# Regrouping the score tiles of a fused attention and mixer kernel from three tiled bursts a step into two

## Chip, cores, metric

One core of one Trainium2 chip. The metric is the device time of the program in microseconds (us), the median of several runs.

## The reference

Attention with squared ReLU in place of softmax, on 8 x 12 heads of 448 positions and 64 channels; its output, with heads side by side, is the input of a mixer block: two matmuls over the positions with a residual, then two over the channels with a residual.

```python
scores = scale * np.matmul(q, k.transpose(0, 1, 3, 2))
attn = np.maximum(scores, 0.0) ** 2 / S
x = (attn @ v) with heads side by side              # 8 x 448 x 768
xt = x.transpose(0, 2, 1)
h = np.maximum(xt @ w_tok1, 0.0) @ w_tok2           # token mixing, 448 -> 256 -> 448
u = x + h.transpose(0, 2, 1)
h2 = np.maximum(u @ w_ch1, 0.0) @ w_ch2             # channel mixing, 768 -> 1536 -> 768
return u + h2
```

## The kernel before

The work is cut into 24 steps of four heads. In a steady step PE computes the scores of step i, the values, token1 and token2 of step i-1, and fills in with channel-mixing units of finished batches. Scores, values and the q/k transposes use the array as four tiles of 64 x 64; everything else uses the whole array. A run of tiled work between full-array work is called a burst below. PE is TensorE, which multiplies matrices into PSUM; ACT (ScalarE) and DVE (VectorE) evict the results, that is, copy them out so that the PSUM buffer is free again; SP issues DMA transfers. x_sb is the transposed x that token1 reads. The parts that matter (cuts marked with `...`):

```python
ps_att = ... tile_pool(name="ps_att", bufs=2, space=PSUM)      # two score buffers of two banks each
ps_acc = ... tile_pool(name="ps_acc", bufs=1, space=PSUM)      # values, q/k transposes, token2
ps_mm  = ... tile_pool(name="ps_mm",  bufs=2, space=PSUM)      # token1, channel units

def scores(i, c):                       # one score tile: four 64x64 matmuls of 448 columns
    ps = ps_att.tile([128, 2, 512], FP32, tag="att", name="sc_ps")
    ...
    nc.scalar.activation(at, ps[:, :, :S], AF.Relu)            # ACT evicts it
    squares.append(at)                                         # DVE squares it later

def fill(share, least=0):               # channel units, paid from a credit
    if not queue:
        return
    credit[0] += share * rate[0]
    done = 0
    while queue and (credit[0] > 0 or done < least):
        cost, unit = queue.pop(0)
        credit[0] -= cost
        unit()
        done += 1
...
for i in range(DB + 1, ND + 2):         # DB = 3, ND = 24; steady from i = 7 on (slow is false)
    slow = i <= 2 * DB
    ...
    scores(i, 0); scores(i, 1)                                 # burst 1
    values(i - 1, range(QC)); values_out(i - 1)
    scores(i, 2)
    ...
    x_back(i - 1)                       # from step 9 on: a DMA transpose of x, needed by token1
    ... u_back(...)                     # DMA transposes of the residual, same SP queue
    square()
    fill(1 / 3)
    scores(i, 3); scores(i, 4)                                 # burst 2
    transposes(i + 1)
    square()
    fill(2 / 9)
    token1(i - 1)
    fill(1 / 9, least=1)
    scores(i, 5); scores(i, 6)                                 # burst 3
    token2(i - 1)
    ...
    square()
    fill(1 / 3)
```

A channel-1 unit is six matmuls evicted by ACT; a channel-2 unit is twelve matmuls evicted by DVE.

Of the kernel before, what the change touches and what calls it, by code (L numbers as in the profile page):

```python
# [16 lines left out]
def kernel(  # L17
# [19 lines left out]
    ND = B * H // 4  # L37
    DB = H // 4
# [88 lines left out]
    def transposes(i, place="acc", split=False):  # L127
        sb = attn.tile([128, 2, 2, S], BF16, name="qkT")
        if place == "att":
            both = ps_att.tile([128, 2, 1024], BF16, tag="att", name="qkT_ps")  # L130
            parts = [both[:, r] for r in range(2)]
        else:
            parts = [ps_acc.tile([128, 1024], BF16, tag=f"acc{r}", name="qkT_ps1") for r in range(2)]
        for w in (1, 0) if i == 0 else (0, 1):
            src = raws.pop((i, "qk"[w]))
            for c in range(QC):
                at = w * S + c * 64
                for r in range(2):
                    h = slice(64 * r, 64 * (r + 1))
                    for g in range(2):  # L140
                        nc.tensor.matmul(  # L141
                            parts[r][64 * g : 64 * (g + 1), at : at + 64],
                            lhsT=src[h, g, c, :],
                            rhs=ident[h, h],
                            is_transpose=True,
                            start=True,
                            stop=True,
                            skip_group_check=True,
                        )
        qkT[i] = sb  # L150
        if place == "att":
            nc.vector.tensor_copy(sb.rearrange("n r w t -> n r (w t)"), both[:, :, : 2 * S])
            return
        for r in range(2):
            (nc.scalar.copy if split and r == 0 else nc.vector.tensor_copy)(  # L155
                sb[:, r].rearrange("n w t -> n (w t)"), parts[r][:, : 2 * S]
            )

    def scores(i, c):
        sb = qkT[i]  # L160
        ps = ps_att.tile([128, 2, 512], FP32, tag="att", name="sc_ps")
        for r in range(2):
            for g in range(2):
                h = slice(64 * g, 64 * (g + 1))
                nc.tensor.matmul(  # L165
                    ps[64 * r : 64 * (r + 1), g, :S],
                    lhsT=sb[h, r, 1, c * 64 : (c + 1) * 64],
                    rhs=sb[h, r, 0, :],
                    start=True,
                    stop=True,  # L170
                    skip_group_check=True,
                )
        at = attn.tile([128, 2, S], BF16, name="at", bufs=12)
        nc.scalar.activation(at, ps[:, :, :S], AF.Relu)  # L174
        squares.append(at)
        at2[i, c] = at

    def square(keep=0):
        while len(squares) > keep:
            at = squares.pop(0)  # L180
            nc.vector.tensor_tensor(out=at, in0=at, in1=at, op=ALU.mult)  # L181
# [38 lines left out]
    x_tiles, r1_tiles, uT_tiles = {}, {}, {}  # L220
    XDMA = 8
# [28 lines left out]
    def token1(i):  # L250
        x_sb = x_tiles.pop(i)
        ps = ps_mm.tile([128, JC, 256], FP32, tag="bank", name="t1_ps")
        for j in range(JC):
            for c in range(4):
                nc.tensor.matmul(  # L255
                    ps[:, j, :],
                    lhsT=wt1[:, c, j * 128 : (j + 1) * 128],
                    rhs=x_sb[:, :, c, :],
                    start=(c == 0),
                    stop=(c == 3),  # L260
                )
        r1 = mix.tile([128, JC, 256], BF16, name="r1_sb")
        nc.scalar.activation(r1, ps, AF.Relu)  # L263
        r1_tiles[i] = r1

    def token2(i, early=False, rs=(0, 1)):
        b, d = divmod(i, DB)
        if d == 0 and b % 2 == 0 and 0 in rs:
            uT_tiles[b // 2] = mix.tile([128, NP, 2 * S], BF16, name="uT_sb")
        r1 = r1_tiles[i]  # L270
        off = (b % 2) * S
        if early:
            parts = {r: ps_mm.tile([128, 512], FP32, tag="bank", name="h_ps1") for r in rs}
        else:
            parts = {r: ps_acc.tile([128, 512], FP32, tag=f"acc{r}", name="h_ps") for r in rs}
        for r in rs:
            for j in range(JC):
                nc.tensor.matmul(  # L278
                    parts[r][:, :S],
                    lhsT=r1[:, j, r * 128 : (r + 1) * 128],  # L280
                    rhs=wt2[:, j, :],
                    start=(j == 0),
                    stop=(j == JC - 1),
                )
        for r in rs:
            nc.vector.tensor_tensor(  # L286
                out=uT_tiles[b // 2][:, 2 * d + r, off : off + S],
                in0=parts[r][:, :S],
                in1=xT[b % 2][:, 2 * d + r, :S],
                op=ALU.add,  # L290
            )
        if 1 in rs:
            u_later.append(i)
# [3 lines left out]
    u_later = []  # L297
# [5 lines left out]
    def u_back(i):  # L303
        b, d = divmod(i, DB)
        t = chunks(b)
        if b not in u_tiles:
            u_tiles[b] = mix.tile([128, NP, NT - NT // 2, 128], BF16, name="u_sb", bufs=3)
        for p in (2 * d, 2 * d + 1):
            nc.sync.dma_start_transpose(
                out=u_tiles[b][:, p, : len(t), :],  # L310
                in_=uT_tiles[b // 2][:, p, t.start * 128 : t.stop * 128],
            )

    def hold_back(b, src):

        u_tiles[b] = mix.tile([128, NP, NT - NT // 2, 128], BF16, name="u_sb", bufs=3)
        for p in range(NP):
            nc.gpsimd.tensor_copy(u_tiles[b][:1, p, 0, :1], src)
# [76 lines left out]
    def channel_work(b):  # L395
        for e in range(2 if b == 0 else 0, EC):
            queue.append((C1, lambda e=e: channel1(b, e)))
        for t in chunks(b):
            for j in range(2):
                later.append((C2, lambda t=t, j=j: channel2(b, t, j)))  # L400
        if b > 0:
            queue.extend(later)
            later.clear()
# [6 lines left out]
    def fill(share, least=0):  # L410
# [9 lines that stand above are left out]
# [74 lines left out]
    i = DB  # L494
# [31 lines left out]
    for i in range(DB + 1, ND + 2):  # L526
        slow = i <= 2 * DB
        if i == 2 * DB + 1:
            rate[0] = (EC * C1 + NT * C2) / DB
        if i < ND:  # L530
            scores(i, 0)
            scores(i, 1)
        if 0 <= i - 1 < ND:
            values(i - 1, range(QC))
            values_out(i - 1)
        if i < ND:
            scores(i, 2)
        if i - 1 < XDMA:
            fill(1 / 3, least=1)
        if 0 <= i - 1 < ND:  # L540
            x_back(i - 1)
        if i > 2 * DB + 1:
            if i == 2 * DB + 2:
                hold_back(1, x_tiles[i - 1][:1, 0, 0, :1])
            while u_later and u_later[0] < i - 1:
                u_back(u_later.pop(0))
        if i + PRE < ND:
            if i - 1 >= XDMA:
                nc.gpsimd.tensor_copy(gate, x_tiles[i - 1][:1, 1, 3, 127:])  # L549
            load_four(i + PRE)  # L550
        if i == 5:
            load_wc2(1, 2)
        square()
        if i - 1 >= XDMA:
            fill(1 / 3)
        if i < ND:
            scores(i, 3)
            scores(i, 4)
        if i + 1 < ND:
            transposes(i + 1)  # L560
        square()
        if not slow:
            fill(2 / 9)
        if 0 <= i - 1 < ND:
            token1(i - 1)
        fill(1 / 3 if slow else 1 / 9, least=1)
        if i < ND:
            scores(i, 5)
            scores(i, 6)
        if 0 <= i - 1 < ND:  # L570
            token2(i - 1)
            if (i - 1) % DB == DB - 1:
                channel_work((i - 1) // DB)
            if i == 2 * DB + 1:
                hold_back(0, uT_tiles[1][:1, 0, :1])
                for _ in range(DB):
                    u_back(u_later.pop(0))
        square()
        fill(1 / 3, least=1 if slow else 0)
    while queue:  # L580
        queue.pop(0)[1]()

# [29 lines left out]
```

## Time and profile before

| | before |
|---|---|
| median time | 380.68 us (380.0 to 380.86) |
| span of the profiled run | 377.8 us |
| PE busy | 365.5 us, 97% |
| DVE, ACT busy | 205.9 us, 213.4 us |
| PE waiting for a score buffer from 76 to 332 us | never |
| PE waiting for x_sb there | 1.4 us in two waits |

PE is the bound and hardly waits in the steady steps. In a timeline row the columns are the start in us, the length in us, engine, line, operation, out<-in, shapes and the count of merged instructions, then in brackets the idle time before it and what ended that.

### The profile page before, as it was taken

The page shows a single profiled execution, that of the slowest core. Times are in us where ns is not written, and L with a number is a line of the kernel's source. Part 1 is how long each engine was busy: PE and PEld are TensorE (multiplying, and loading weights), DVE is VectorE, ACT ScalarE, POOL GpSimd, SP SyncE. Part 2 cuts the span into 40 slices and gives each one's busy share as a digit, 9 for nine tenths or more (in the row PEclk, how much of TensorE's full clock was granted, in tenths as well). Part 3 has the DMA queues.
Part 4 walks back from the last instruction along what each step waited for, and adds up shares of the span by engine and source line. Part 5 has one row for each costly group of instructions (what it writes and reads, how often), then busy time and mean ns, then how long its engine had stood idle before and what let it go on. Part 6 is the DMA issues. An engine that isn't in the chain of part 4 may idle for free.

```text
span 377.8 us, 10082 instructions
## 1 busy us (share of the span) xinstructions
PE 365.5 (97%) x4335; PEld 200.7 (53%) x4335; DVE 205.9 (54%) x371; ACT 213.4 (56%) x297; POOL 100.9 (27%) x186
## 2 busy tenths in 40 slices
PE   8888999999989999999999999999999999999995
PEld 3444455555555564565555554555545654555563
DVE  2876688764567665465555575466555664121021
ACT  4996888877434457745676347654676446412400
POOL 8974548212330321430321304303300000000000
PEclk9999999999999999999999999999999999999999
DMA  8989999933988866846835898738550344333024
GB/s 153 121 118 203 193 206 170 183 45 71 150 146 163 160 137 111 108 79 136 154 65 72 146 139 139 112 61 171 97 103 17 74 115 87 57 69 85 0 61 107
DMA packets 69325, 43.30 MB, mean 115 GB/s; under 512 B 43360, under 2 KB 65824, under 8 KB 69280
## 3 DMA queue, kind: packets, MB, share of 16 engines
q0 software_dynamic: 24416, 21.47, 39.8%
q1 hardware_dynamic: 44560, 20.75, 26.0%
q8 instruction: 34, 0.56, 0.6%
q10 hardware_dynamic: 304, 0.43, 0.4%
q14 instruction: 11, 0.09, 0.1%
HBM read 43.38 MB, written 11.01 MB: 144 GB/s over the span
## 4 chain that ended last, share of the span: by engine, by line
PE 88%; DVE 4%; ACT 4%; DMA 3%; issue 1%; SPq 0%; ACTq 0%
PE m_ps L327 28%; PE m_ps L366 27%; PE sc_ps L165 9%; PE acc_ps L193 8%; PE t_ps L255 6%; PE h_ps L278 5%; DMA x_sb<-xT 3%; ACT at L174 3%; PE qkT_ps L141 3%; DVE uT_sb L286 1%; PE warm_ps L429 1%; DVE at L181 1%; PE m_ps L345 1%; DVE xT L211 1%; PE x_ps L237 1%
## 5 line engine op out<-in xcount | busy, mean ns | idle before, releaser
L174 ACT ACTIVATE at<-sc_ps 128x896 bf16<-128x896 f32 x168 | 145.1, 920 | 59.3 <-PE sc_ps L165 59.0
L327 PE MATMUL m_ps<-uT_sb,wc 128*128 128x448 bf16 x564 | 115.6, 353 | 0.2 <-DVE uT_sb L286 0.2
L366 PE MATMUL m_ps<-wc,r_sb 128*128 128x384 bf16 x672 | 115.2, 326 | 0.0
L181 DVE TENSOR_TENSOR at<-at 128x896 bf16<-128x896 bf16 x168 | 96.8, 619 | 7.6 <-ACT at L174 7.6
L366 PEld LDWEIGHTS <-r_sb 128*128 128x128 bf16 x672 | 64.3, 98 | 45.6 <-issue 3.9
L334 ACT ACTIVATE r_sb<-m_ps 128x448 bf16<-128x448 f32 x94 | 51.2, 544 | 60.1 <-PE m_ps L327 59.8
L327 PEld LDWEIGHTS <-wc 128*128 128x128 bf16 x564 | 53.3, 98 | 49.8 <-issue 4.3
L373 DVE TENSOR_TENSOR out_sb<-m_ps,u_sb 128x384 f32<-128x384 f32 x56 | 31.1, 556 | 60.6 <-PE m_ps L366 59.6
L165 PE MATMUL sc_ps<-qkT 64*64 64x448 bf16 x672 | 52.7, 360 | 2.9 <-ACT at L174 2.2
L286 DVE TENSOR_TENSOR uT_sb<-h_ps,xT 128x448 bf16<-128x448 f32 x48 | 27.8, 620 | 39.5 <-PE h_ps L278 39.5
L211 DVE TENSOR_SCALAR xT<-acc_ps 128x448 bf16<-128x448 f32 x45 | 26.1, 620 | 34.8 <-PE acc_ps L193 34.8
L193 PE MATMUL acc_ps<-at,v_raw 64*64 64x448 bf16 x672 | 38.6, 350 | 0.0
L549 POOL COPY gate<-x_sb 1x1 bf16<-1x1 bf16 x12 | 2.3, 193 | 126.2 <-DMA x_sb<-xT 126.2
L83 POOL DMA_DIRECT2D q_raw<-in_q_dram x48 | 29.0, 615 | 20.0 <-DMA wc<-in_moe_w_ch_dram 16.9
L165 PEld LDWEIGHTS <-qkT 64*64 64x64 bf16 x672 | 15.6, 105 | 30.8 <-issue 26.6
L83 POOL DMA_DIRECT2D v_raw<-in_v_dram x48 | 29.5, 636 | 7.2 <-DMA wc<-in_moe_w_ch_dram 4.6
L155 DVE COPY qkT<-qkT_ps 128x896 bf16<-128x896 bf16 x39 | 22.6, 619 | 14.9 <-PE qkT_ps L141 14.9
L83 POOL DMA_DIRECT2D k_raw<-in_k_dram x46 | 28.1, 630 | 0.1
L255 PE MATMUL t_ps<-x_sb,wt 128*128 128x256 bf16 x192 | 25.0, 273 | 2.1 <-DMA x_sb<-xT 1.4
L193 PEld LDWEIGHTS <-v_raw 64*64 64x64 bf16 x672 | 20.2, 107 | 12.1 <-issue 0.8
L263 ACT ACTIVATE r_sb<-t_ps 128x512 bf16<-128x512 f32 x24 | 14.3, 597 | 20.7 <-PE t_ps L255 20.6
L278 PE MATMUL h_ps<-wt,r_sb 128*128 128x448 bf16 x96 | 22.6, 355 | 0.0
(40 smaller groups left out, 122.0 us busy)
## 6 DMA issues: line engine op xcount, KB each, us to landing
out_dram<-out_sb SPq DMA_DIRECT2D x54, 192.0 KB, 3.3
q_raw<-in_q_dram POOLq DMA_DIRECT2D x48, 112.0 KB, 4.3
v_raw<-in_v_dram POOLq DMA_DIRECT2D x48, 112.0 KB, 5.4
k_raw<-in_k_dram POOLq DMA_DIRECT2D x46, 112.0 KB, 5.5
wc<-in_moe_w_ch_dram POOLq DMA_DIRECT2D x4, 1152.0 KB, 11.0
u_sb<-uT_sb SPq DMA_TRANSPOSE x48, 2.6
x_sb<-xT SPq DMA_TRANSPOSE x16, 3.3
k_first<-in_k_dram SPq DMA_DIRECT2D x1, 224.0 KB, 3.5
```

What stands on the lines that cost most here:

```text
L83: eng.dma_start(out=dst[64 * r : 64 * (r + 1)].rearrange("p g c d -> p g (c d)"), in_=src[b, h0 : h0 + 2].rearrange("g (p c) d -> p g (c d ...
L165: nc.tensor.matmul(ps[64 * r : 64 * (r + 1), g, :S], lhsT=sb[h, r, 1, c * 64 : (c + 1) * 64], rhs=sb[h, r, 0, :], start=True, stop=True, s ...
L174: nc.scalar.activation(at, ps[:, :, :S], AF.Relu)
L181: nc.vector.tensor_tensor(out=at, in0=at, in1=at, op=ALU.mult)
L193: nc.tensor.matmul(ps[r][64 * g : 64 * (g + 1), :S], lhsT=v_raw[h, g, c, :], rhs=at[h, g, :], start=(c == 0), stop=(c == QC - 1), skip_gro ...
L255: nc.tensor.matmul(ps[:, j, :], lhsT=wt1[:, c, j * 128 : (j + 1) * 128], rhs=x_sb[:, :, c, :], start=(c == 0), stop=(c == 3),)
L278: nc.tensor.matmul(parts[r][:, :S], lhsT=r1[:, j, r * 128 : (r + 1) * 128], rhs=wt2[:, j, :], start=(j == 0), stop=(j == JC - 1),)
L286: nc.vector.tensor_tensor(out=uT_tiles[b // 2][:, 2 * d + r, off : off + S], in0=parts[r][:, :S], in1=xT[b % 2][:, 2 * d + r, :S], op=ALU.add,
L327: nc.tensor.matmul(ps[:, :S], lhsT=wc1[:, g, e * 128 : (e + 1) * 128], rhs=uT[:, g, off : off + S], start=(g == 0), stop=(g == CC - 1),)
L334: nc.scalar.activation(r2[:, e, off : off + S], ps[:, :S], AF.Relu)
L366: nc.tensor.matmul(ps[:, :HN], lhsT=r2[:, e, t * 128 : (t + 1) * 128], rhs=wc2[:, e, cols], start=(e == 0), stop=(e == EC - 1),)
L373: nc.vector.tensor_tensor(out=o[:, cols].rearrange("n (g d) -> n g d", d=128), in0=ps[:, :HN].rearrange("n (g d) -> n g d", d=128), in1=u_ ...
```

## The change

The intent is to leave and enter tiled mode twice a step instead of three times: score 3 joins the first burst, score 6 goes behind the transposes, scores 4 and 5 stand ahead of them. Fill shares are redistributed (they still sum to 1 a step, but to 4/3 in steps 7 and 8). A second part issues one pair of residual transposes a step later, so that fewer of them stand in the SP queue ahead of the first x transpose.

```diff
--- before.py
+++ after.py
@@ -535,6 +535,8 @@
             values_out(i - 1)
         if i < ND:
             scores(i, 2)
+            if not slow:
+                scores(i, 3)
         if i - 1 < XDMA:
             fill(1 / 3, least=1)
         if 0 <= i - 1 < ND:
@@ -542,7 +544,7 @@
         if i > 2 * DB + 1:
             if i == 2 * DB + 2:
                 hold_back(1, x_tiles[i - 1][:1, 0, 0, :1])
-            while u_later and u_later[0] < i - 1:
+            while u_later and u_later[0] < max(i - 1 - (i == 2 * DB + 2), 0):
                 u_back(u_later.pop(0))
         if i + PRE < ND:
             if i - 1 >= XDMA:
@@ -551,19 +553,39 @@
         if i == 5:
             load_wc2(1, 2)
         square()
-        if i - 1 >= XDMA:
-            fill(1 / 3)
+        if not slow:
+            fill(0.45, least=2)
+            if i < ND:
+                scores(i, 4)
+                scores(i, 5)
+            if i + 1 < ND:
+                transposes(i + 1)
+            if i < ND:
+                scores(i, 6)
+            square()
+            fill(0.1)
+            if 0 <= i - 1 < ND:
+                token1(i - 1)
+            fill(0.1, least=1)
+            if 0 <= i - 1 < ND:
+                token2(i - 1)
+                if (i - 1) % DB == DB - 1:
+                    channel_work((i - 1) // DB)
+            if i == 2 * DB + 1:
+                hold_back(0, uT_tiles[1][:1, 0, :1])
+                for _ in range(DB):
+                    u_back(u_later.pop(0))
+            fill(0.35)
+            continue
         if i < ND:
             scores(i, 3)
             scores(i, 4)
         if i + 1 < ND:
             transposes(i + 1)
         square()
-        if not slow:
-            fill(2 / 9)
         if 0 <= i - 1 < ND:
             token1(i - 1)
-        fill(1 / 3 if slow else 1 / 9, least=1)
+        fill(1 / 3, least=1)
         if i < ND:
             scores(i, 5)
             scores(i, 6)
@@ -571,12 +593,8 @@
             token2(i - 1)
             if (i - 1) % DB == DB - 1:
                 channel_work((i - 1) // DB)
-            if i == 2 * DB + 1:
-                hold_back(0, uT_tiles[1][:1, 0, :1])
-                for _ in range(DB):
-                    u_back(u_later.pop(0))
         square()
-        fill(1 / 3, least=1 if slow else 0)
+        fill(1 / 3, least=1)
     while queue:
         queue.pop(0)[1]()
 
```

## The prediction

> **What bounds the kernel now.** I read the page first, then PE's waits in the steady stretch, then the timelines of PE and ACT over one steady step. The page:
>
> ```profile
> PE 365.5 (97%) x4335; PEld 200.7 (53%) x4335; DVE 205.9 (54%) x371; ACT 213.4 (56%) x297; POOL 100.9 (27%) x186
> PEclk9999999999999999999999999999999999999999
> ...
> L174 ACT ACTIVATE at<-sc_ps 128x896 bf16<-128x896 f32 x168 | 145.1, 920 | 59.3 <-PE sc_ps L165 59.0
> L334 ACT ACTIVATE r_sb<-m_ps 128x448 bf16<-128x448 f32 x94 | 51.2, 544 | 60.1 <-PE m_ps L327 59.8
> ```
>
> PE is busy for 97% of the span at full clock. No other engine passes 56%, so PE's instruction stream sets the time: a microsecond that PE idles or loses is a microsecond of the kernel. ACT needs 920 ns per score tile (168 of them, seven per step) and 544 ns per channel-1 unit. PE's waits between 76 and 332 us, which hold the steady steps but for the first few microseconds of the first, are a single row:
>
> ```profile
> PE t_ps L255 <- DMA x_sb<-xT: 1.4, 2, 1.2
> ```
>
> So now PE never waits for a score buffer there. It waits twice for a residual transpose (1.19 us at 109 us, 0.24 us at 227 us). That no score wait exists is the fact that the change puts at risk. The PE timeline of one steady step:
>
> ```profile
> 166.26 0.57 PE L165 MATMUL sc_ps<-qkT 64*64 64x448 bf16 x8
> 166.66 0.39 PE L141 MATMUL qkT_ps<-ident,q_raw 64*64 64x64 bf16 x28
> 166.88 0.43 PE L141 MATMUL qkT_ps<-ident,k_raw 64*64 64x64 bf16 x28
> 167.25 2.12 PE L366 MATMUL m_ps<-wc,r_sb 128*128 128x384 bf16 x12
> 169.21 1.04 PE L255 MATMUL t_ps<-x_sb,wt 128*128 128x256 bf16 x8
> 170.11 2.11 PE L366 MATMUL m_ps<-wc,r_sb 128*128 128x384 bf16 x12
> 172.15 0.57 PE L165 MATMUL sc_ps<-qkT 64*64 64x448 bf16 x8
> 172.65 0.93 PE L278 MATMUL h_ps<-wt,r_sb 128*128 128x448 bf16 x4
> 173.42 2.11 PE L366 MATMUL m_ps<-wc,r_sb 128*128 128x384 bf16 x12
> 175.46 0.57 PE L165 MATMUL sc_ps<-qkT 64*64 64x448 bf16 x8
> 175.87 1.49 PE L193 MATMUL acc_ps<-at,v_raw 64*64 64x448 bf16 x28
> 177.19 0.36 PE L165 MATMUL sc_ps<-qkT 64*64 64x448 bf16 x4
> ```
>
> Three tiled (64*64) bursts a step stand between full-array work. The reader should look at starts, because the ends are modelled. Twelve m_ps matmuls followed by more full-array work take 1.96 us (167.25 to 169.21); followed by a burst they take 2.04 us (170.11 to 172.15). Individual starts in the trace give 256 against 163 ns for the last one: 0.09 us to enter a burst. Two score tiles followed by tiled work take 0.40 us (166.26 to 166.66); followed by full-array work 0.50 us (172.15 to 172.65): 0.10 us to leave. A burst costs about 0.195 us besides its work. The ACT timeline gives when score buffers come free:
>
> ```profile
> 160.79 2.53 ACT L174 ACTIVATE at<-sc_ps 128x896 bf16<-128x896 f32 x3
> 166.70 1.73 ACT L174 ACTIVATE at<-sc_ps 128x896 bf16<-128x896 f32 x2 [3.38 <-PE sc_ps L165]
> ```
>
> With ACT idle the first eviction starts 0.44 us after the score tile does (166.26 to 166.70) and takes 0.92, so its buffer is free at +1.35; the second follows 0.81 later, free at +2.17 (0.44 + 1.73). If the work before the burst was a channel-1 unit, ACT evicts that first: the burst of 160.24 had its first eviction start at 160.79, 0.55 after, and everything is 0.11 later (+1.46 and +2.27). There are only two score buffers, and the startup shows what happens when they run out:
>
> ```profile
> 14.65 0.38 PE L165 MATMUL sc_ps<-qkT 64*64 64x448 bf16 x4
> 15.46 0.38 PE L165 MATMUL sc_ps<-qkT 64*64 64x448 bf16 x4
> 16.27 0.38 PE L165 MATMUL sc_ps<-qkT 64*64 64x448 bf16 x4
> ```
>
> Score tiles then start every 0.81 us, ACT's pace, each 0.05 us after the end of the eviction of two tiles earlier.
>
> **What the Trainium skill says.** "TensorEngine Tiling (Array Packing)", section Key Properties: a change of tiling mode drains the array. The trace agrees: 0.09 us in, 0.10 us out. "TensorE: Matmul & The Clock Gate", section Step-by-step: only weight loads are pulled ahead, the matmuls stay in program order. So a score tile that waits holds back all full-array work behind it; the startup rows fit that. "ScalarE: Activation LUTs", section What ACT_TABLE_LOAD costs: an activation with immediates takes 186 ns plus 0.833 ns per element, and neighbours overlap by about 93 ns. For 896 elements that is 932 and 839 ns; the trace has 920 and 0.81 us. "Perfetto Trace Analysis", section Optimization Strategy: the same gap repeating on the engine that should be saturated can mean too few buffers. The trace before has no such gap; I expect the one after to have it.
>
> **The change part by part.** Steps i = 7 to 23 (17 of them) go from bursts of three score tiles around the values, two ahead of the transposes, and two alone, to: scores 0 and 1, values, scores 2 and 3; and scores 4 and 5, transposes, score 6. PE's matmuls are the same in number and shape, only reordered; the order listing of the changed program confirms that, and that scores 2 and 3 each carry a wait on ACT.
>
> Removed: one burst a step. 17 x 0.195 = 3.3 us saved.
>
> Added, first burst, counted from its start: scores 0 and 1 take 0.40, values 1.32, score 2 starts at 1.73 (buffer 0 free at 1.35 or 1.46: no wait, as today). Score 3 would start at 1.94, but its buffer is free at 2.17 + 0.05 = 2.22, or 2.32 after a channel-1 unit. PE waits 0.28 or 0.38 us. Working the fill credit through the program gives a channel-1 unit just before this burst in 11 of the 17 steps, a channel-2 unit (evicted by DVE) in 6: 11 x 0.38 + 6 x 0.28 = 5.9 us.
>
> Added, second burst: scores 4 and 5 take 0.40, transposes 0.48, so score 6 could start at 0.88. Buffer 4 is free at 1.35 + 0.05 = 1.40, or 1.51 after channel 1. PE waits 0.52 or 0.63. The credit gives 11 steps after channel 2 and 5 after channel 1; in step 23 there are no transposes, so score 6, ready at 0.43, waits until 1.51, that is 1.08. 11 x 0.52 + 5 x 0.63 + 1.08 = 9.9 us.
>
> Moved: the fill shares still sum to 1.0 a step (four thirds in steps 7 and 8, so a few channel units run earlier and the tail holds fewer; the same PE work). The queue never empties in the steady part in either version. In five steps the 0.1 fill ahead of token1 is empty, so token1 follows score 6 directly. Its x_sb must have landed by then: two channel-2 units (3.9 us) and the second burst still stand between, token1 starts about 6.3 us after the end of the values, and the transposes land 4.4 to 4.7 us after it in most steps (6.0 and 6.6 in two with heavy loading). So little is lost there.
>
> Residual transposes: at step 8 one pair fewer is queued on SP ahead of step 9's x_sb transpose, whose issue today falls 1.64 us after the values instead of 1.25, landing late. With that, and with more PE work between, the two waits for x_sb go: 1.4 us saved.
>
> Sum: -3.3 - 1.4 + 5.9 + 9.9 = +11.1 us, all on PE and so on the path. 380.68 + 11.1 gives 391.8 us, 2.9% slower.
>
> **The rivals.** (a) The author's hope: values and transposes give ACT time to free the buffers, so waits vanish and only the burst saving counts: 380.7 - 3.3 - 1.4 = 376.0 us. Against it: the buffer of score 1 comes free at +2.17 after the burst's start, in today's trace, while score 3 would be due at +1.94; and 0.48 us of transposes do not cover the 0.92 us of an eviction. For it: only that the pauses in the design were put where ACT needs them. (b) Burst waits half as long as I count, because something that I take as lost (the drain into full-array work, the wait for x_sb) hides inside them: +15.8 x 0.5 - 4.7 = +3.2, 384 us. Against it: starts alone were used, and the drain comes after score 6, not in its wait. (c) More waits than I count: token2's weights wait for r1, which ACT now evicts behind scores 5 and 6. I get r1 ready at about 3.55 us after the second burst's start and token2 due at 3.7 where only one channel-1 unit stands between: 0.15 us of room. If it misses by 0.5 us in the five steps with the empty fill, or x_sb lands late there, +2 to 3 us: 394 us.
>
> **Range and chances.** The waits come from start times and durations that repeat from step to step within 0.02 us, so the sum is good to some 2 us either way if the mechanism holds: 388.5 to 394.5 us. A slowdown of over 2% needs more than 388.3 us, that is 70% of my net sum; I give it 0.86. Within 2%: 0.12, mostly (b). Faster by 2% is beyond even (a): 0.02.
>
> **What would show it.** PE's waits should have a new row, score tiles waiting for ACT's evictions, about 34 times and near 16 us in total, none of them over 1.1 us; PE's busy share falls to some 93%, with PE's busy time down by about 2 to 4 us. Score 3 should start 2.2 to 2.3 us and score 6 1.4 to 1.5 us after their burst's first tile. x_sb's row should be gone from the waits of PE. I am wrong if that score row is under 8 us, if the saving per burst is not near 0.2 us, or if a row of token2 waiting for r1, or of token1 for x_sb, exceeds 2 us.

## The result

The changed kernel takes 391.37 us (391.17 to 391.69, four runs) against 380.56 us before (380.0 to 380.86) in the same rounds: a ratio of 1.0286, 95% interval 1.0269 to 1.0304. Ratios here are the mean time of one kernel's fast runs over that of the other's fast runs of the same rounds, so not quite the ratio of the medians that are quoted. The profiled spans are 389.8 and 377.8 us; they differ by more than the medians because the profiled run of the kernel before took 379.59 us, less than any of the four runs of its median.

The page after, with PE's busy share and the two groups concerned (the number after the second bar is the idle time of the engine just before these instructions):

```profile
PE 367.8 (94%) x4335; PEld 205.4 (53%) x4335; DVE 206.7 (53%) x371; ACT 211.6 (54%) x297; POOL 99.8 (26%) x186
...
L174 ACT ACTIVATE at<-sc_ps 128x896 bf16<-128x896 f32 x168 | 143.1, 924 | 65.5 <-PE sc_ps L165 65.2
...
L165 PE MATMUL sc_ps<-qkT 64*64 64x448 bf16 x672 | 56.0, 361 | 13.3 <-ACT at L174 12.0
```

PE runs the same 4335 matmuls in a longer span. The idle time ahead of the score matmuls was 2.9 us before, all in the startup; now it is 13.3 us, 12.0 of it ended by ACT's evictions in waits of over 0.15 us. ACT itself is idle for longer than before (65.5 against 59.3 us ahead of its evictions): it is late in each burst without being busy overall.

PE's waits after, from 76 to 345 us (total us, times, longest):

```profile
PE sc_ps L165 <- ACT at L174: 9.4, 27, 0.9
PE m_ps L366 <- DVE out_sb L373: 0.3, 1, 0.3
PE m_ps L327 <- ACT r_sb L334: 0.2, 1, 0.2
```

The row for x_sb has gone and a row for score buffers has come. One steady step after, PE:

```profile
171.97 0.57 PE L165 MATMUL sc_ps<-qkT 64*64 64x448 bf16 x8
172.38 1.49 PE L193 MATMUL acc_ps<-at,v_raw 64*64 64x448 bf16 x28
173.70 0.87 PE L165 MATMUL sc_ps<-qkT 64*64 64x448 bf16 x8
174.50 4.07 PE L366 MATMUL m_ps<-wc,r_sb 128*128 128x384 bf16 x24
178.51 0.57 PE L165 MATMUL sc_ps<-qkT 64*64 64x448 bf16 x8
178.91 0.39 PE L141 MATMUL qkT_ps<-ident,q_raw 64*64 64x64 bf16 x28
179.13 0.43 PE L141 MATMUL qkT_ps<-ident,k_raw 64*64 64x64 bf16 x28
179.91 0.38 PE L165 MATMUL sc_ps<-qkT 64*64 64x448 bf16 x4 [0.35 <-ACT at L174]
```

and ACT in the same stretch:

```profile
172.41 3.43 ACT L174 ACTIVATE at<-sc_ps 128x896 bf16<-128x896 f32 x4 [4.33 <-PE sc_ps L165]
178.94 1.73 ACT L174 ACTIVATE at<-sc_ps 128x896 bf16<-128x896 f32 x2 [3.10 <-PE sc_ps L165]
```

Scores 2 and 3 (the row at 173.70) need 0.80 us from start to the next full-array matmul at 174.50, where two score tiles used to take 0.50 (172.15 to 172.65 in the prediction's timeline). Score 6 starts at 179.91, 1.40 us after its burst's first tile, though the transposes begin at 178.91 and take 0.48 us. The chain of work that ended last (start, length, what) passes through ACT at this place, where before it stayed on PE:

```profile
178.58 0.34 PE sc_ps L165 x4
178.92 0.02 issue
178.94 0.93 ACT at L174
179.87 0.04 issue
179.91 0.38 PE sc_ps L165 x4
```

One reading trap: the idle time in the wait row is smaller than what PE lost. Score 3 has an idle time of 0.13 or 0.23 us, but from score 2's start to score 3's start there are 0.49 or 0.59 us where 0.21 would do (the time between the first two tiles of a burst). The modelled end of the tile before counts the first 0.16 us or so of each wait as busy: for 34 waits 5.4 us, which less the 3.3 us of the saved bursts is near the 2.3 us by which PE's busy time rose with the same work. The six waits of 0.13 us are missing from the row altogether.

### The profile page after: what moved, and what is told of

Same layout as the page of the kernel before. It is cut to its first block, busy times and chain, and to the rows that moved or that the text cites.

```text
span 389.8 us, 10078 instructions
## 1 busy us (share of the span) xinstructions
PE 367.8 (94%) x4335; PEld 205.4 (53%) x4335; DVE 206.7 (53%) x371; ACT 211.6 (54%) x297; POOL 99.8 (26%) x186
## 4 chain that ended last, share of the span: by engine, by line
PE 76%; ACT 11%; issue 6%; DVE 3%; POOL 2%; DMA 1%; ACTq 0%; POOLq 0%; DVEq 0%
PE m_ps L366 28%; PE m_ps L327 28%; ACT at L174 10%; PE sc_ps L165 7%; PE t_ps L255 5%; PE h_ps L278 4%; PE acc_ps L193 2%; DVE uT_sb L286 1%; DVE at L181 1%; POOL q_raw L83 1%; DMA wt<-in_moe_w_tok_dram 1%; PE m_ps L345 1%; PE qkT_ps L141 1%; ACT x_sb L246 1%; POOL wt L96 1%
## 5 line engine op out<-in xcount | busy, mean ns | idle before, releaser
L174 ACT ACTIVATE at<-sc_ps 128x896 bf16<-128x896 f32 x168 | 143.1, 924 | 65.5 <-PE sc_ps L165 65.2
L165 PE MATMUL sc_ps<-qkT 64*64 64x448 bf16 x672 | 56.0, 361 | 13.3 <-ACT at L174 12.0
L165 PEld LDWEIGHTS <-qkT 64*64 64x64 bf16 x672 | 20.5, 104 | 43.4 <-issue 38.1
```

The source lines that it names most:

```text
L165: nc.tensor.matmul(ps[64 * r : 64 * (r + 1), g, :S], lhsT=sb[h, r, 1, c * 64 : (c + 1) * 64], rhs=sb[h, r, 0, :], start=True, stop=True, s ...
```

## The experiments

My theory was that of the prediction: PE waits for score buffers behind ACT, against a small saving per burst. The rivals were that the transposes' new place on the SP queue, the redistributed fill, or something in longer bursts made the difference.

### One part of the change alone: the residual transposes

```diff
 (kernel before)
-            while u_later and u_later[0] < i - 1:
+            while u_later and u_later[0] < max(i - 1 - (i == 2 * DB + 2), 0):
```

> The kernel before with only the residual transposes spread by a step (three bursts kept). My theory: only the 1.19 us wait of token1 for x_sb in step 9 goes, so about 379.4 us, 0.3% faster than before; the 0.24 us wait of step 17 stays. Rival (the spread of transposes is what made the changed kernel slow, by pushing DMA work into step 9): slower than before by several us.

Measured: 379.25 us against 379.74 before, ratio 0.9982 (0.9966 to 0.9998). The direction fits. The gain is smaller than the 1.2 us that I expected: 0.5 us by the medians and by the spans (377.3 against 377.8); the interval, 0.02 to 0.34%, just holds the expected 0.3%. The mechanism fits only in part. PE's waits from 76 to 345 us:

```profile
PE t_ps L255 <- DMA x_sb<-xT: 1.0, 1, 1.0
```

The transpose of step 9 was issued 1.25 us after the values instead of 1.64, as expected, yet it took 4.93 us to land, where most x transposes take 3.2 to 3.3. So the wait shrank from 1.19 to 0.95 us and did not go. In this run step 17's wait of 0.24 us was gone instead.

### The other part alone: the bursts

```diff
 (kernel after)
-            while u_later and u_later[0] < max(i - 1 - (i == 2 * DB + 2), 0):
+            while u_later and u_later[0] < i - 1:
```

> The changed kernel with the residual transposes issued as before, so only the two bursts and the fill shares differ from before. My theory: 391.4 us, the same as the changed kernel within 0.3 us, because token1 of step 9 now starts 8.3 us after the values and x_sb lands 6.4 us after them. Rival: at least 1 us away from the changed kernel, in either direction.

Measured: 391.60 us, ratio to before 1.0306; span 389.7 against 389.8 us for the whole change, with the same row of score waits (9.4 us, 27 times). Bursts and fill make the whole difference; the spread of the transposes is worth nothing in the changed kernel, because token1 there comes late enough anyway: in step 9 of this run x_sb landed 2.8 us ahead of it.

### Score 3 alone, and the last-but-one tile behind the transposes alone

```diff
 (kernel before; first run)                     (kernel before; second run)
             scores(i, 2)                                    transposes(i + 1)
+            if not slow:                       +        if not slow and i < ND:
+                scores(i, 3)                   +            scores(i, 5)
 ...                                            ...
-            scores(i, 3)                       -            scores(i, 5)
+            if slow:                           +            if slow:
+                scores(i, 3)                   +                scores(i, 5)
             scores(i, 4)                                    scores(i, 6)
```

Both keep three bursts and the fill shares of before.

> The kernel before with score 3 alone moved up behind score 2, still three bursts. My theory: score 3 waits 0.28 us (9 steps) or 0.38 us (8 steps) for score 1's eviction, 5.6 us, leaving the burst after a wait costs 0.02 us more, and about 0.5 us of the x_sb waits go: 386 us (385 to 387), with score 3 starting 2.2 to 2.3 us after its burst's first tile. Rival (ACT keeps up because the values stand between, and the loss of the changed kernel comes from the fill shares): 380.5 us.

Measured: 387.54 us against 379.74 before, ratio 1.0201 (1.0177 to 1.0226). Score 3 started 2.21 us after its burst's first tile in 9 steps and 2.32 in 8, so the mechanism and its size are as expected; the total is 1.5 us above the middle of what I wrote and so outside my range of 385 to 387. The profiled run shows an accident on top:

```profile
113.36 1.49 PE L255 MATMUL t_ps<-x_sb,wt 128*128 128x256 bf16 x8 [2.73 <-DMA x_sb<-xT]
114.64 3.39 PE L366 MATMUL m_ps<-wc,r_sb 128*128 128x384 bf16 x12
```

In step 9, x_sb was late by 2.73 us (its transpose was issued 3.8 us after the values, behind 14 residual transposes), and from 113.81 to 117.22 us, by the trace's clock record, the clock was at half, so twelve matmuls took 3.39 us instead of about 2.1. The two runs at a clock of 0.995 and 0.996 took 388.9 and 388.2 us; the two at 1.0 and 0.999 took 386.8. These two lie 7.1 us above the kernel before, where the waits and the slower exits come to 5.9 by starts; whether a late x_sb is in them too is not shown, since they were not profiled.

> The kernel before with score 5 alone moved up behind the transposes, still three bursts (the third has one tile). My theory: score 5 waits 0.52 us (10 steps), 0.63 us (6) or about 0.97 us (the step without transposes) for score 3's eviction, 9.9 us, and part of the x_sb waits goes: 390 us (389 to 391). Rival (the transposes cover the eviction): 380.5 us.

Measured: 389.33 us, ratio 1.0243 (1.0226 to 1.0261), inside the range. Score 5 started 1.40 us after its burst's first tile in 11 steps and 1.51 in 6, as computed. PE's waits from 76 to 345 us:

```profile
PE sc_ps L165 <- ACT at L174: 7.1, 17, 0.8
PE t_ps L255 <- DMA x_sb<-xT: 1.2, 1, 1.2
```

Each half of the regrouping costs by itself about what the sum gave it (the first half somewhat more, see above), with no change of fill.

### Taking the suspected cost away: half evictions

Wrong results: from step 7 on, ACT evicts one head of a score tile instead of two, and the values read it twice. PE's instructions stay.

```diff
 (kernel after, and kernel before as control)
-        nc.scalar.activation(at, ps[:, :, :S], AF.Relu)
-        squares.append(at)
+        if i > 2 * DB:
+            nc.scalar.activation(at[:, 0, :], ps[:, 0, :S], AF.Relu)
+        else:
+            nc.scalar.activation(at, ps[:, :, :S], AF.Relu)
+        squares.append(at[:, 0, :] if i > 2 * DB else at)
 ...
-                        rhs=at[h, g, :],
+                        rhs=at[h, 0 if i > 2 * DB else g, :],
```

> Wrong result on purpose: the changed kernel, but in steps 7 on ACT evicts and DVE squares only one head of each score tile (448 elements, about 0.54 us instead of 0.92) and the values read that head twice; PE's matmuls are the same. My theory: buffers come free sooner, score 3 never waits, score 6 waits only 0.15 to 0.26 us (0.7 in step 23), some 4 us in all instead of 15.8: 379 us (378 to 380.5), a little below before. Rival (the loss comes from the fill shares or from the longer bursts themselves, not from waits for score buffers): it stays at 390 us or above.

Measured: 378.98 us, ratio to before 0.9958 (0.9930 to 0.9985). This is 12.4 us below the changed kernel (in other rounds), and by starts the waits fall from 15.8 to 3.6 us. The fill shares and the order of the bursts are those of the changed kernel, so neither costs this time by itself. PE's row of score waits from 76 to 345 us is down to the one step without transposes:

```profile
PE sc_ps L165 <- ACT at L175: 0.6, 1, 0.6
```

Score 3 no longer waits. Score 6 started at 1.03 and 1.14 us, as computed from 0.54 us per eviction, where 0.88 was possible; these waits are too short for the row. The second burst of one step, where the whole eviction had put score 6 at 1.40:

```profile
173.47 0.57 PE L165 MATMUL sc_ps<-qkT 64*64 64x448 bf16 x8
...
174.50 0.38 PE L165 MATMUL sc_ps<-qkT 64*64 64x448 bf16 x4
```

> Wrong result on purpose, the control for the run above: the kernel before with the same halved evictions in steps 7 on. My theory: no score tile waited for a buffer there, so nothing is gained: 380.5 us within 0.6. Rival (less ACT and DVE work speeds up any version): several us faster than before, so that the run above would say nothing on the waits.

Measured: 379.29 us against 380.06 before, ratio 0.9965 (0.9937 to 0.9993). That is 1.2 us below the 380.5 that I wrote and so outside my 0.6, but only 0.8 below the median of before in the same rounds, where three of the eleven runs took over 381 us. The control holds for its purpose: halving the evictions does 0.8 us by the medians (2.4 us at most by the interval) for the kernel before and about 12.4 us for the one after.

### Taking away one of the two waits, with a right result

```diff
 (kernel after)
-        nc.scalar.activation(at, ps[:, :, :S], AF.Relu)
+        if i > 2 * DB and c == 1:
+            nc.vector.tensor_scalar(
+                out=at, in0=ps[:, :, :S], scalar1=0.0, scalar2=None, op0=ALU.max
+            )
+        else:
+            nc.scalar.activation(at, ps[:, :, :S], AF.Relu)
```

> The changed kernel, right result, with score 1 of steps 7 on evicted by DVE (a maximum with zero, about 1.1 us) beside ACT's eviction of score 0. My theory: buffer 1 is free about 1.8 us after the burst's start, score 3 is due at 1.94 and no longer waits, score 6 waits as before: 5.9 us less and some 0.4 us of slower leaving, so 385.2 us (384.3 to 386). Rival (DVE, at 53% already, then becomes late for the values' eviction or the squares and its own waits eat the gain): 390 us or more.

Measured: 385.22 us, as expected to the hundredth by chance, ratio 1.0124 (1.0083 to 1.0165). The same step's score rows:

```profile
171.25 0.55 PE L165 MATMUL sc_ps<-qkT 64*64 64x448 bf16 x8
...
177.14 0.38 PE L165 MATMUL sc_ps<-qkT 64*64 64x448 bf16 x4 [0.35 <-ACT at L179]
```

Scores 2 and 3 go back to 0.55 us from 0.87; score 6 still waits. DVE, at 58% now, adds no row to PE's waits.

### The cost of a burst by itself

```diff
 (kernel before)
             scores(i, 5)
-            scores(i, 6)
+            if slow:
+                scores(i, 6)
         if 0 <= i - 1 < ND:
             token2(i - 1)
+            if not slow and i < ND:
+                scores(i, 6)
```

> The kernel before with score 6 behind token2 instead of beside score 5, so four bursts a step and no score tile nearer to its buffer's eviction. My theory: one more way into and out of a tiled burst in 17 steps, 17 x 0.195 = 3.3 us: 383.9 us (383.3 to 384.5). Rival (a burst's entry and exit are hidden or only a matter of the modelled ends): 380.5 us.

Measured: 384.25 us, ratio 1.0106 (1.0073 to 1.0139), span 381.7 against 377.8 us. PE's waits are those of before, so the time is the bursts'. Adding up the start-to-start times at entries and exits gives 3.7 us for 17 bursts, 0.22 each against my 0.195: leaving a burst that is one tile long takes some 0.02 us more.

### A better version: two misses, then two gains

The numbers say how far bursts can be merged with two score buffers: two tiles ahead of the transposes, three around the values on ACT alone, four if DVE evicts the second. So every other step can do with two bursts, if the seventh tile of one step shares a burst with the first of the next. In the diffs, `on_dve` means that DVE evicts the tile, as in the run of score 1 above. I first tried to remove the x_sb waits too, with a minimum of two channel units ahead of token1 in each step, and the mixed bursts on top of it.

```diff
 (kernel before with the spread; first run)
-            fill(2 / 9)
+            fill(2 / 9, least=2)
 (second run, in addition)
+        n0 = 0 if slow or i % 2 else 1
-            scores(i, 0); scores(i, 1)
+            scores(i, n0); scores(i, n0 + 1, on_dve=not slow)
 ...
-            scores(i, 2)
+            scores(i, n0 + 2)
+            if not slow: scores(i, n0 + 3)
 ...
-            scores(i, 3); scores(i, 4)
+            scores(i, 3 if slow else n0 + 4); scores(i, 4 if slow else n0 + 5)
 ...
-            scores(i, 5); scores(i, 6)
+            if slow: scores(i, 5); scores(i, 6)
+            elif n0 == 0: scores(i, 6); scores(i + 1, 0)       # where there is a step i + 1
```

> A right kernel meant to gain: the kernel before with the transposes spread and at least two channel units between the second burst and token1, so that x_sb has landed in steps 9 and 17 too; three bursts. My theory: both x_sb waits (1.4 us together) go, nothing else moves: 378.6 us (378 to 379.3). Rival (the wait comes back as a wait of token2 for r1, or the late landing is later than 2 us): no gain beyond the 0.5 us that the spread alone gave.

Measured: 381.63 us against 380.59, ratio 1.0021 (0.9994 to 1.0048): a miss. Both x_sb waits went, but the credit paid for the forced unit by leaving the last fill of some steps empty. There the third burst and the next step's first stood with token2 alone between:

```profile
114.48 0.93 PE L278 MATMUL h_ps<-wt,r_sb 128*128 128x448 bf16 x4
115.38 0.38 PE L165 MATMUL sc_ps<-qkT 64*64 64x448 bf16 x4
116.18 0.38 PE L165 MATMUL sc_ps<-qkT 64*64 64x448 bf16 x4 [0.42 <-ACT at L174]
```

Six such waits, 2.5 us in the row: the fault of the change, made again by way of the fill.

> A right kernel meant to gain: the run above, and every other steady step has two bursts, laid so that no score tile comes before its buffer is free: four tiles around the values (the second one evicted by DVE), two ahead of the transposes, and in the other steps the seventh tile shares a burst with the first tile of the next step. My theory: 8 bursts fewer at 0.195 us, 1.6 us below the run above, no row of score tiles waiting for ACT: 377.1 us (376.3 to 378). Rival (DVE's evictions are late when a channel-2 sum precedes them, or they delay the values' eviction and with it x_sb): no faster than the run above, with new waits for DVE or x_sb.

Measured: 381.52 us, ratio 1.0018 (0.9988 to 1.0048), a miss for the same reason: in three steps the last fill was empty, with waits of 0.42 us for ACT and 0.26 us for DVE. By itself this run looks like the rival that I had named, new waits for DVE and no gain over the run before; the next two, with the fill set right, speak against it:

```diff
 (third run: the mixed bursts with the spread and fill(2 / 9) as before; fourth run, on top of it)
-            fill(2 / 9)
+            fill(2 / 9, least=2 if i in (9, 17) else 0)
 ...
-        fill(1 / 3, least=1 if slow else 0)
+        fill(1 / 3, least=1 if slow or i in (9, 17) else 0)
```

> The mixed bursts with the spread transposes and the fill shares of the kernel before, since the minimum of two units ahead of token1 emptied the last fill of some steps and so ran two bursts together. My theory: 8 bursts fewer at 0.195 us, 1.6 us, and some 0.5 us of the spread, less 0.5 us for one wait for a channel-2 sum on DVE in step 8: 0.4% below before (0.3 to 0.6%), no row of score tiles waiting. Rival (the mixed order costs as much elsewhere as it saves): the same as before within 0.15%.

> The run above with one channel unit moved ahead of token1 in steps 9 and 17 alone, where x_sb lands late, and one unit kept at those steps' ends so that no bursts run together. My theory: the remaining x_sb waits (about 1.0 us) go as well: 0.65% below before (0.5 to 0.85%). Rival (the unit taken from the next step's first fill opens a new wait for x_sb or for a score buffer there): no better than the run above.

Measured: 378.24 us (378.17 to 378.40) and 377.48 us (377.39 to 377.69), both with right results, ratios 0.9915 (0.9885 to 0.9945) and 0.9896 (0.9868 to 0.9923). That is 0.85% and 1.04% below before, more than I had written (0.3 to 0.6% and 0.5 to 0.85%). The ratios may flatter: the kernel before ran at 379.7 to 382.8 us in these rounds, six of its eleven runs with a clock of 0.993 to 0.996. Against the mean of its five runs at 0.997 and above, 380.23 us, the means of the two versions (378.26 and 377.51) are 0.5% and 0.7% below, in my ranges; but I chose these five after seeing the result. If the low clocks came from the kernel's own wait for x_sb, as in the profiled run of score 3 alone, the full ratios would be the fair ones; no run before of these rounds was profiled, so that is open. PE's waits of the fourth version from 76 to 345 us:

```profile
PE m_ps L371 <- DVE out_sb L378: 0.5, 1, 0.5
```

No score wait and no x_sb wait is left. This version beats both kernels, by a few tenths of a per cent over before and by 3.5% over the changed one (377.48 against 391.37 us, of different rounds).

## Why the prediction was right

The net sum was +11.1 us, the medians say +10.8 and the profiled spans +12.0 (11.8 from the first burst of step 7 on). That the medians agree to 0.3 us is partly luck, as the terms below show. Term by term, by start-to-start times in the trace after:

| term | predicted | measured |
|---|---|---|
| 17 bursts fewer | -3.3 us | -3.3 from entries and exits before; an added burst costs 0.22 instead of 0.195 us |
| score 3 waits | +5.9 us | +5.8: 11 x 0.38 + 6 x 0.27 |
| score 6 waits | +9.9 us | +10.0: starts at 1.40 in 11 steps, 1.51 in 6, where 0.88 (0.43 in the last step) was possible |
| x_sb waits | -1.4 us | -1.8: the row has gone, and by starts the two waits had cost 1.35 and 0.40 us |
| leaving a burst whose last tile waited | not seen | +0.8: 34 exits at 0.316 instead of 0.292 us |

These sum to +11.5 us. Of the rest, two short waits in steps 7 and 8, ahead of channel units, are in the trace after alone (0.18 and 0.26 us of idle time).

The prediction put score 3, without a wait, at 1.94 us. The runs with halved evictions and with DVE put it at 1.92: a score tile takes 0.19 us, and the 0.02 above that belong to the burst. Read so, score 3 costs 6.2 us and a burst 0.22, as in the run with four bursts; the sum of the two terms stays the same.

- **Bound.** PE set the time before and after; each lost tenth on it showed in the total.
- **Two score buffers and ACT's 0.92 us.** Right, and shown: each half alone costs its share (387.5 and 389.3 us), shorter evictions remove the loss (379.0 us), and a second evicting engine removes score 3's part alone (385.2 us).
- **Saving per burst.** Right in size, by the run with four bursts (0.22 us each). With most of the waits gone the two-burst kernel falls just below before; against its control (379.29 us) the gain is 0.3 us, since 3.6 us of waits are left.
- **Rivals.** The author's hope (a) fell with the first row of waits. The half-hidden wait (b) fell: nothing hides in them. A late token2 or x_sb (c) did not come; no wait of either is in the list, and x_sb landed at least 1.5 us ahead of token1.
- **Residual transposes.** The step was half wrong. I wrote that the spread and the later token1 together would end the x_sb waits. They did, but the later token1 does it without the spread (the run of the bursts alone has no x_sb row), and the spread alone takes 0.24 us off step 9: it mends the issue, while the transfer took 4.9 us to land there. In the changed kernel the same transfer took 3.2 us; why they differ is not shown. (The prediction says at one place that PE waits for a residual transpose; its waits are those of token1 for x_sb.)
- **Wrong signs named beforehand.** I expected about 16 us in the row of score waits and less PE busy time. The row shows 9.4 us in the steady stretch and busy time rose. The loss is 15.8 us by starts; the row counts only what lies past a tile's modelled end.

## What to carry to other kernels

Before merging bursts to save mode changes, count how many tiles the evicting engine can free in the time that the burst lasts: the n-th tile of two buffers starts no sooner than the end of the eviction of tile n-2, here 1.40 and 2.22 us after the burst's start. Full-array work between bursts is not only a cost of two mode changes but also the time in which buffers come free, and a fill that pays by credit can close such a gap unseen. Judge waits of a pipelined engine by start-to-start times against the same pair of instructions elsewhere, not by the idle column.

## What the Trainium skill lacked or had wrong

- "TensorEngine Tiling (Array Packing)", Key Properties, says that a mode change drains the array but gives no figure. Here entering costs 0.09 us and leaving 0.10 us, 0.13 us after a tile that had waited, and a whole added one-tile burst 0.22 us.
- "TensorE: Matmul & The Clock Gate", Part 1, has the clock fall to half after an idle window of about 3.4 us, and calls the window free-running. In the run of score 3 alone the changes of the clock lie at 4.58, 113.81 and 117.22 us, 32 windows of 3.413 us and then one apart, which fits a free-running window. But in the window that ended at 113.81 PE idled for only 2.73 us, and the clock still fell for the next 3.41 us: an idle stretch shorter than the window can be enough. How much is needed, one case does not tell.
- "Perfetto Trace Analysis" says in its part on the Tensor Engine instruction that the profiler estimates a matmul's end, and in Optimization Strategy tells to look for gaps on the bounding engine; it does not say that a gap therefore understates a wait. Here 34 waits with 10.4 us of gaps (down to 0.13 us each) cost 15.8 us by starts.
- No page that I read tells how far the landing of a DMA transpose scatters within one kernel: in the kernel before, most x transposes landed 3.2 to 3.3 us after their issue, three of them 4.8 to 5.4 us (five of the sixteen landings are not in the trace).
